# A decode block of attention and MLP on one core: two small side loads behind the fifth K unit, and a bias in one transfer

## Chip, core and metric

One core of a Trainium2 chip runs the program alone. The metric is the device time of one execution in microseconds (us), the median over several runs. Beside these times there is one profiled execution, with a record of every instruction and of every DMA packet. A core has TensorE (PE in the profile), VectorE (DVE), ScalarE (ACT), GpSimd (POOL) and SyncE (SP), and sixteen DMA engines that move the data. A transfer is issued on a queue, here SP's or ACT's, and is cut into packets that the DMA engines carry.

## What is computed

Two tokens (batch 2, one position, width 576) pass through a layer norm; then attention over a window of a key/value cache and an MLP run on the same normalized input, and both are added to `x`:

```python
def _A_ref(x, k_cache, v_cache, wq, wo):
    ...
    W = min(4096, max(256, Sk // 4))          # 2048 of 8192 positions
    q = (x @ wq)...                           # 32 heads of 128
    k = jnp.repeat(k_cache[:, :, Sk - W:, :], rep, axis=1)   # 16 kv heads, rep = 2
    v = jnp.repeat(v_cache[:, :, Sk - W:, :], rep, axis=1)
    scores = jnp.einsum("bhqd,bhkd->bhqk", q, k) * (Dh ** -0.5)
    p = _softmax(scores, axis=-1)
    o = jnp.einsum("bhqk,bhkd->bhqd", p, v)
    return ... @ wo

def _B_ref(x, w1, b1, w2, b2):
    h = jnp.einsum("bsd,df->bsf", x, w1) + b1                # 576 -> 4608
    r = jnp.where(h > zero, h, zero)
    return jnp.einsum("bsf,fd->bsd", r * r, w2) + b2

return x + _A_ref(xn, ...) + _B_ref(xn, ...)
```

All inputs are bf16. Some 53.6 MB are read: the windows of the K and V caches (16.8 MB each), `wq`, `wo` (4.7 MB each), `w1` and `w2` (5.3 MB each).

## The kernel before

The cache is cut into eight units (`NU = 8`), one for four kv heads of one batch row; a unit of K or V is a tile of 128 partitions with 16,384 bytes in each, loaded by one DMA (`issue_kv`, L105). Six such tiles (`kvpool`, `bufs=6`) are used in turn by K and V units. `wq`, `w1` and `wo` share one buffer (`wbig`, `issue_flat`, L118), so that `w1` can only be loaded after the queries are made, and `wo` only after the first MLP product.

Everything large is issued on SP's queue, in the order of the program: k0, wq, k1, v0, k2, v1, k3, v2, k4, v3, k5, v4, k6, v5, w1, k7, v6, v7, wo, and `w2` in five parts (w2a L435, w2b L436, w2c in three pieces L438, `W2P`). An SP issue waits for what its buffer's last user has to finish (PE, for a K or V tile), and for a semaphore: the transfers of the program take eight completion semaphores in turn, and a transfer can be issued only when the transfer that had the same semaphore eight places earlier has landed. ACT's queue carries the small ones: `x` (L124), the first MLP bias `b1_sb` (L415, three transfers of three, three and two rows of 1,152 bytes), the second bias (L416, one row) and half of the output (L474; L472 writes the same place once beforehand).

`step(u)` handles one unit: PE transposes K in eight groups (`kT_ps`, L96), ACT and DVE copy them to SBUF (L269, L271), `scores` and `softmax` follow, and the product with V of the unit two places back (`pv`, L93) lies between. `mlp_h` multiplies by `w1` (`h_ps`) after step 6, then the program issues `wo` and `w2`, runs step 7 and the last two `pv`, and sums everything into `out_ps`: first `wo` (tile `ws`), then `w2a`, `w2b`, three matmuls into an unused tile (`spin_ps`), and `w2c`. ACT copies `out_ps` to `fin_sb` (L473) and two DMAs write the output.

`w2c_sb` (L209) is allocated at the start, in a pool of its own, 128 partitions of nine rows of 576 numbers; it stays empty until the three pieces of L438 are loaded, late in the program.

Of the kernel before, what the change touches and what calls it, by code (L numbers as in the profile page):

```python
# [16 lines left out]
def kernel(  # L17
# [14 lines left out]
    nc = tc.nc  # L32
    P = 128
    B, Sq, D = A_x.shape
# [57 lines left out]
    def matmul(*a, **k):  # L92
        tc.keep_in_program_order(nc.tensor.matmul(*a, **k))  # L93
# [8 lines left out]
    def issue_kv(tiles, cache, u, name):  # L102
        tq, b = divmod(u, B)
        tl = kvpool.tile([P, UE], BF16, tag="kv", name=f"{name}_{u}")
        nc.sync.dma_start(out=tl[:], in_=cache[b, tq * TH:(tq + 1) * TH, S0:Sk, :].rearrange(  # L105
            "h (c j) d -> c h (j d)", c=CP))
        tiles[u] = tl

    def load_k(u):
        issue_kv(k_tiles, A_k_cache, u, "k")  # L110
# [67 lines left out]
    for t0, half, k0, n, pc in ((0, 0, 0, NK, 0), (0, 1, 0, NK, 1), (1, 0, 1, NK - 1, 1), (1, 1, 0, NK - 1, 0)):  # L178
# [11 lines left out]
                          in_=own[:].unsqueeze(2).to_broadcast([P, NC, WC]))  # L190
# [11 lines left out]
                          in_=ident[0:2 * NG4, 0:2 * NG4].rearrange("p (x g) -> p x g", g=NG4).unsqueeze(3)  # L202
# [5 lines left out]

    w2c_sb = w2pool.tile([P, (FR - R9) * D], BF16, name="w2c")  # L209

    out_ps = psum.tile([RO, HD], F32, tag="out", name="out_ps")
    nc.vector.memset(out_ps[:], 0.0)

    def out_acc(lhsT, rhs, o, start=False, stop=False, acc=out_ps, base=0):
        for i in range(2):
            p = base + 32 * i
            matmul(acc[p:p + B, :], lhsT=lhsT, rhs=rhs[:, o * D + i * HD:o * D + (i + 1) * HD], start=start,
                   stop=stop, skip_group_check=True, tile_position=(0, p))
# [165 lines left out]
    def step(u):  # L384
        fin = None
        w = u - 2
        with_pv = w >= 0
        for g in range(NG):
            transposes(u, g)
            if with_pv and g == 1:  # L390
                pv(w, 0, 2)
            if with_pv and g == 2:
                pv(w, 1, 2)
                fin = pv_end(w)
            if g == TG + 1:
                scores(u, 0)
            if g == TG + 2 and fin:
                fin()
        scores(u, 1)
        softmax(u)  # L400
# [10 lines left out]
    softmax(0)  # L411
    load_v(2)
    b1_rows = B_b1.rearrange("(x n) -> x n", n=HW)
    for i0, i1 in ((0, 3), (3, 6), (6, 8)):
        nc.scalar.dma_start(out=b1_sb[i0:i1, :], in_=b1_rows[i0:i1, :])  # L415
    nc.scalar.dma_start(out=xb_sb[B:B + 1, :], in_=B_b2.rearrange("(o n) -> o n", o=1))  # L416
    step(1)
    load_k(4)
    out_acc(sel_b[:], xb_sb, 0, start=True)
    for u in range(2, NU - 1):  # L420
        step(u)
# [84 lines left out]
```

## Time and profile before

| | |
|---|---|
| time, median of 3 runs | 133.90 us (133.72 to 133.91) |
| the profiled execution's own time | 133.77 us |
| its span | 131.9 us |
| PE busy | 86.9 us (66%) |
| DVE busy | 63.0 us (48%) |
| ACT busy | 46.7 us (35%) |
| DMA | 53.74 MB, mean 407 GB/s over the span |
| chain that ended last | DMA 77%, PE 17% |

The span goes from the program's first to its last instruction; the time has some 1.9 us more around it. The profile's views are: the busy time of each engine; the chain of work that ended last, followed back from the last instruction; busy time in stretches, with the share of the sixteen DMA engines that was busy; the queues with their packets; the waits of each queue; and, in the trace itself, each DMA packet with its queue, start, duration and size, and the landings of each transfer, sixteen for a transfer that all engines share.

The DMA share of the span in 40 equal slices, in tenths:

```profile
DMA  3999989999999999999999999999999989899970
```

### The profile page before, as it was taken

To read this page: it belongs to the slowest core of one execution; us is meant where nothing else is said; L and a number is where in the kernel's file an instruction comes from. 1 tells how busy PE (TensorE), PEld (TensorE's weight loads), DVE (VectorE), ACT (ScalarE), POOL (GpSimd) and SP (SyncE) were. 2 spreads that over 40 slices of the span, in tenths; PEclk is the share of its full clock that TensorE was granted. 3 is DMA by queue.
4 is the path that set the end of the run, shared out by engine and by line. 5 is a ranking of instruction groups with operands and counts; after the bars stand their busy time and mean duration, and the time that the engine had idled before them with its cause. 6 is when DMAs were issued, how large, how long until landed. Compare 5 with 4: busy or idle time off the path is not lost.

```text
span 131.9 us, 2023 instructions
## 1 busy us (share of the span) xinstructions
PE 86.9 (66%) x818; PEld 50.9 (39%) x818; DVE 63.0 (48%) x176; ACT 46.7 (35%) x68; POOL 4.2 (3%) x14
## 2 busy tenths in 40 slices
PE   0079419599589597599687699203919972729672
PEld 0069302287345353445353354002518630215241
DVE  6764400344657677457677457620072677550000
ACT  5715500339576094255094346010014532000101
POOL 2000000010010100100100100100010001000000
PEclk9999955959999999779999869855595999555999
DMA  3999989999999999999999999999999989899970
GB/s 120 432 443 493 403 383 427 407 462 403 455 412 442 427 407 462 407 442 427 432 437 400 457 479 428 407 415 423 427 427 442 504 374 492 380 421 399 409 285 1
DMA packets 3498, 53.74 MB, mean 407 GB/s; under 512 B 401, under 2 KB 546, under 8 KB 802
## 3 DMA queue, kind: packets, MB, share of 16 engines
q1 hardware_dynamic: 3460, 53.61, 95.4%
q8 instruction: 6, 0.10, 0.3%
q10 hardware_dynamic: 30, 0.02, 0.0%
q14 instruction: 2, 0.02, 0.0%
HBM read 53.62 MB, written 0.00 MB: 407 GB/s over the span
## 4 chain that ended last, share of the span: by engine, by line
DMA 77%; PE 17%; SPq 1%; DVE 1%; ACT 1%; issue 1%; ACTq 0%; DVEq 0%
DMA w<-in_B_w_dram 24%; DMA w2c<-in_B_w_dram 24%; DMA k<-in_A_k_cache_dram 16%; DMA wq<-in_A_wq_dram 13%; PE kT_ps L96 7%; PE h_ps L93 3%; PE q_ps L93 3%; PE sc_ps L93 1%; PE o_ps L93 1%; PE out_ps L93 1%; DVE qrow L237 1%; SPq L105 0%; ACT qrow L237 0%; DVE qz L253 0%; SPq L435 0%
## 5 line engine op out<-in xcount | busy, mean ns | idle before, releaser
L96 PE MATMUL kT_ps<-ident_f,k 128*128 128x128 f32 x256 | 42.0, 315 | 5.5 <-DMA k<-in_A_k_cache_dram 4.4
L96 PEld LDWEIGHTS kT_ps<-ident_f,k 128*128 128x128 f32 x256 | 33.3, 162 | 19.1 <-issue 10.2
L269 ACT COPY kT<-kT_ps 128x1024 bf16<-128x1024 bf16 x32 | 31.9, 1012 | 19.6 <-PE kT_ps L96 19.4
L271 DVE COPY kT<-kT_ps 128x1024 bf16<-128x1024 bf16 x32 | 21.8, 681 | 7.1 <-PE kT_ps L96 6.7
L93 PE MATMUL sc_ps<-kT,qz 128*32 128x512 bf16 x128 | 9.7, 383 | 6.7 <-DVE kT L271 4.7
L301 ACT ACTIVATE p<-sc_ps,bias 128x512 bf16<-128x512 f32 x8 | 5.5, 687 | 21.3 <-DVE gown L297 15.0
L93 PE MATMUL o_ps<-v,pT 128*32 128x512 bf16 x128 | 11.9, 455 | 0.0
L93 PEld LDWEIGHTS <-xnT 128*4 128x4 bf16 x108 | 3.6, 121 | 15.8 <-issue 14.2
L93 PE MATMUL h_ps<-w,xnT 128*4 128x288 bf16 x72 | 4.3, 431 | 7.2 <-DMA w<-in_B_w_dram 7.2
L304 DVE STREAM_TRANSPOSE pT<-p 128x512 bf16<-128x512 bf16 x8 | 5.7, 710 | 6.2 <-ACT p L301 6.2
L332 DVE SCALAR_TENSOR_TENSOR o<-o_ps,in_s,o 128x128 f32<-128x128 f32 x24 | 8.2, 344 | 0.4
L290 DVE TENSOR_REDUCE m<-sc_ps 128x1 f32<-128x512 f32 x8 | 5.5, 691 | 4.7 <-PE sc_ps L93 4.7
L93 PE MATMUL q_ps<-wq,xnT 128*4 128x512 bf16 x36 | 4.0, 628 | 4.6 <-DMA wq<-in_A_wq_dram 4.6
L372 DVE TENSOR_TENSOR hrow<-t 100x1152 bf16<-100x1152 f32 x2 | 2.6, 1355 | 8.9 <-ACT t L370 8.9
L93 PE MATMUL op_ps<-o,of_h 128*32 128x129 f32 x16 | 3.7, 316 | 4.6 <-DVE o L332 4.6
L93 PEld LDWEIGHTS <-qz 128*32 128x32 bf16 x128 | 2.1, 94 | 10.4 <-DVE kT L271 7.2
L294 POOL PARTITION_ALL_REDUCE gmax<-m x8 | 2.9, 366 | 93.6 <-DVE m L292 93.6
L96 PE MATMUL pro_ps<-ident,xn_sb 2*128 2x2 bf16 x5 | 0.9, 181 | 6.8 <-DVE xn_sb L169 6.5
L330 DVE TENSOR_SCALAR o<-o_ps,in_s 128x128 f32<-128x128 f32 x8 | 2.7, 342 | 4.7 <-PE o_ps L93 4.7
L458 ACT COPY pre_sb<-pre_ps 34x288 f32<-34x288 f32 x1 | 0.4, 393 | 12.6 <-PE pre_ps L93 12.6
L93 PE MATMUL out_ps<-wo,ws 128*2 128x288 bf16 x32 | 4.0, 443 | 1.1 <-DVE ws L348 1.1
L237 DVE CAST qrow<-q_ps 100x512 bf16<-100x512 f32 x1 | 0.7, 692 | 8.0 <-PE q_ps L93 8.0
(76 smaller groups left out, 61.2 us busy)
## 6 DMA issues: line engine op xcount, KB each, us to landing
k<-in_A_k_cache_dram SPq DMA_DIRECT2D x8, 2048.0 KB, 21.6
v<-in_A_v_cache_dram SPq DMA_DIRECT2D x8, 2048.0 KB, 33.6
w<-in_B_w_dram SPq DMA_DIRECT2D x1, 5184.0 KB
wq<-in_A_wq_dram SPq DMA_DIRECT2D x1, 4608.0 KB, 17.7
wo<-in_A_wo_dram SPq DMA_DIRECT2D x1, 4608.0 KB
w2a<-in_B_w_dram SPq DMA_DIRECT2D x1, 2592.0 KB
w2b<-in_B_w_dram SPq DMA_DIRECT2D x1, 1296.0 KB, 29.5
w2c<-in_B_w_dram SPq DMA_DIRECT2D x1, 864.0 KB
```

Of the source, the lines that this page charges most:

```text
L93: tc.keep_in_program_order(nc.tensor.matmul(*a, **k))
L96: tc.keep_in_program_order(nc.tensor.transpose(*a, **k))
L237: cp(out=qrow[:, k * QW:(k + 1) * QW].rearrange("p (i a d) -> p i a d", a=2, d=Dh), in_=q_ps[0:RB, k * QW // 2:(k + 1) * QW // 2].rearrang ...
L269: nc.scalar.copy(out=kT, in_=kT_ps[:])
L271: nc.vector.tensor_copy(out=kT, in_=kT_ps[:])
L290: nc.vector.tensor_reduce(out=m1[:], in_=sc_ps[:], axis=AX.X, op=ALU.max)
L294: nc.gpsimd.partition_all_reduce(gmax[:], m2[:], channels=P, reduce_op=ReduceOp.max)
L301: nc.scalar.activation(out=p_sb[:], in_=sc_ps[:], func=ACT.Exp, bias=bias[:, 0:1], scale=scale, accum_out=o1[:, Dh:Dh + 1])
L304: nc.vector.transpose(out=pT[:].rearrange("p j r -> p (j r)"), in_=p_sb[:])
L330: nc.vector.tensor_scalar(scalar1=in_s[:, 0:1], scalar2=None, op0=ALU.mult, **kw)
L332: nc.vector.scalar_tensor_tensor(scalar=in_s[:, k:k + 1], in1=o1[:, 0:Dh], op0=ALU.mult, op1=ALU.add, **kw)
L372: nc.vector.tensor_tensor(out=h4[:, :, k * HB:(k + 1) * HB], in0=t4, in1=t4, op=ALU.mult)
```

## The change

Two things are edited. The first MLP bias comes in one transfer of eight rows instead of three transfers. And after `load_k(4)` two transfers more are issued on SP's queue, by a new function `side_load(k, a0, c0)`. It reads from `w2`, seen as rows of 4,608 bytes (`w_rows`), `k` groups of six rows starting at row `a0`, of each group the first four; and writes them to `4 * k` partitions of `w2c_sb`, 4,608 bytes in each, from column `c0` on. `side_load(5, 0, 0)` fills partitions 0 to 19, `side_load(2, 32, 4 * D)` partitions 0 to 7 beside it. What they write is not read: the three pieces of L438 load all of `w2c_sb` as before. So 28 rows of 4,608 bytes, 0.13 MB, are read more.

```diff
     w2c_sb = w2pool.tile([P, (FR - R9) * D], BF16, name="w2c")
+
+    w_rows = B_w2.rearrange("(a r) n -> a (r n)", r=4)
+
+    def side_load(k, a0, c0):
+        nc.sync.dma_start(out=w2c_sb[0:4 * k, c0:c0 + 4 * D],
+                          in_=w_rows[a0:a0 + 6 * k, :].rearrange("(g i) n -> g i n", g=k)[:, 0:4, :])
...
     b1_rows = B_b1.rearrange("(x n) -> x n", n=HW)
-    for i0, i1 in ((0, 3), (3, 6), (6, 8)):
+    for i0, i1 in ((0, 8),):
         nc.scalar.dma_start(out=b1_sb[i0:i1, :], in_=b1_rows[i0:i1, :])
     nc.scalar.dma_start(out=xb_sb[B:B + 1, :], in_=B_b2.rearrange("(o n) -> o n", o=1))
     step(1)
     load_k(4)
+    side_load(5, 0, 0)
+    side_load(2, 32, 4 * D)
     out_acc(sel_b[:], xb_sb, 0, start=True)
```

The instructions of PE, DVE and POOL stay what they are, in the same order. ACT has two DMA issues less, SP two more. Because the completion semaphores are handed out in turn, the transfers behind the bias take other semaphores than before.

## The prediction

> **What bounds the kernel now.** I read the chain of waits first, then busy time by stretches, then the DMA queues, then what the SP queue waits for, and last the single DMA packets of the trace.
>
> ```profile
> 59.38 31.73 DMA w<-in_B_w_dram
> ...
> 91.14 4.35 PE h_ps L93 x72
> ...
> 96.84 31.09 DMA w2c<-in_B_w_dram
> 127.93 0.04 issue
> 127.97 1.37 PE out_ps L93 x18
> ```
>
> The columns are start, length, what. The end follows the last transfers: w2c, then 1.37 us of matmuls. The one stretch of computing in the last 70 us, 4.35 us of `h_ps`, counts only if the DMA engines run dry under it. The stretches say whether they do (last two columns: share of the 16 DMA engines that is busy, and GB/s):
>
> ```profile
> 2.50:20.00 17.50, 8.01 (x49) 6.70 (x53) 8.09 (x30) 7.41 (x10) 0.00 (x0) 0.90 0.99 420
> 20.00:60.00 40.00, 32.46 (x278) 18.99 (x270) 21.53 (x55) 19.10 (x29) 1.46 (x4) 0.87 1.01 430
> 60.00:91.00 31.00, 19.56 (x165) 10.22 (x164) 17.37 (x45) 11.99 (x16) 1.10 (x3) 0.85 1.00 429
> 91.00:125.00 34.00, 23.40 (x297) 13.16 (x297) 14.49 (x37) 6.66 (x13) 0.70 (x2) 0.74 1.00 429
> 126.50:127.00 0.50, 0.50 (x12) 0.35 (x7) 0.00 (x0) 0.00 (x0) 0.00 (x0) 1.00 0.93 362
> 127.00:127.25 0.25, 0.25 (x6) 0.11 (x2) 0.00 (x0) 0.00 (x0) 0.00 (x0) 1.00 0.68 270
> 127.25:127.50 0.25, 0.25 (x3) 0.12 (x2) 0.00 (x0) 0.00 (x0) 0.00 (x0) 1.00 0.45 171
> 127.50:128.00 0.50, 0.35 (x4) 0.05 (x4) 0.00 (x0) 0.00 (x0) 0.00 (x0) 1.00 0.46 176
> 128.00:128.50 0.50, 0.50 (x10) 0.36 (x11) 0.00 (x0) 0.00 (x0) 0.00 (x0) 1.00 0.36 127
> 128.50:128.75 0.25, 0.25 (x9) 0.22 (x6) 0.00 (x0) 0.00 (x0) 0.00 (x0) 1.00 0.04 14
> ```
>
> The engines are full from 2.5 to 125 us, at 429 to 430 GB/s from 20 us on. They do not stop together: from 127.25 us seven of sixteen (0.45) still work, from 128 six (0.36). The trace's landings of the last w2c piece show it one by one: eight engines between 127.28 and 127.61 us, two at 128.09, six between 128.75 and 128.99. The kernel ends when the slowest engine does, so the question is which engines are late, and why.
>
> ```profile
> q1 hardware_dynamic: 3460, 53.61, 95.4%
> q8 instruction: 6, 0.10, 0.3%
> q10 hardware_dynamic: 30, 0.02, 0.0%
> q14 instruction: 2, 0.02, 0.0%
> ```
>
> Six instruction fetches of 16,384 bytes (q8) and two of 8,192 (q14): six engines very late, two half late. In the packet records a q8 fetch starts where one engine's q1 packet ends (at 29.68, 48.90, 68.34, 84.53, 106.48 and 123.18 us), takes 0.88 to 0.96 us, and the q1 packet beside it grows from 0.61 to 1.09; after each, one more of the sixteen landings is some 1.5 us late. The q14 fetches (35.48 and 69.68 us) cost some 0.8. No engine is hit twice.
>
> **Which engine is hit.** Between two hits every engine sends one 16,384-byte packet each 0.607 us, so the sixteen keep their phases: 0, 29, 32, 34, 48, 52, 61, 70, 77, 116, 163, 169, 202, 213, 282 and 373 ns behind the earliest. The small ACT-queue packets (q10, 1,152 bytes) name three of them: the two b1 transfers of three rows put one packet on three engines each (8.80, 8.89, 8.94 us), the transfer of two rows on two of these (14.35, 14.49), the one-row b2 on one (17.12). Followed to the phases, engine "first" (four packets) is the one at 77, "second" (three) at 163, "third" (two) at 61. The q8 fetches hit 282, 48, 34, 70, 116 and one of 202 and 213; the q14 fetches 0 and 163. So first and third have slack, and **the second is one of the two that land at 128.09**.
>
> **The change, part by part.** *One b1 transfer instead of three.* ACT issues two DMAs less (0.98 us for three, before); its next work, `rstd`, leads to `xnT`, which waits for wq until 19.14 us anyway, so nothing is gained at the end. On the engines eight rows go one each to eight engines instead of 3, 3 and 2. One such packet costs its engine 0.053 us (the next q1 packet starts 47 ns late, and the one after the completion write 6). First and second save two, 0.11 us, third saves one, five others gain one. If b1 landed later, nothing is near: its matmul runs at 83.5 us.
>
> *The SP queue.* The semaphores of the transfers go round in order, eight in all, so two transfers less shift what each SP issue waits for.
>
> ```profile
> SPq L105 <- PE kT_ps L96: 29.9, 6, 9.3
> ...
> SPq L105 <- DMA k<-in_A_k_cache_dram: 12.1, 2, 7.1
> SPq L105 <- DMA b_sb<-in_B_b_dram: 6.4, 3, 2.3
> ```
>
> The 6.4 us of waiting for b1 go: v0, k2, v1 and k3 are issued sooner. v2 then waits for wq (19.14 us) and goes some 2.8 us later than its 16.37. Neither matters: at 19 us k1, v0, k2, v1 and k3 stand in the queues, 5 x 2.1 MB, 24 us at 430 GB/s. k4 (issued 33.41) waits for `kT_ps` as now. The two side loads are issued behind it, some 0.55 us each, before v3, whose own wait ends at 38.31: 4.4 us of room for 1.1. Behind v3 stand the later loads, each with 10 us and more of queue ahead of it. w1 will wait for k4's landing (54.54 us, issue at 59.38), k7 and v6 for the side loads' landing (about 55, issues at 62.61 and 67.20): all past by then. wo, issued after `h_ps` at 95.51, has cover until the v units land, 104.0 to 105.6 us. Cost: nothing.
>
> *The side loads themselves.* 20 + 8 packets of 4,608 bytes, read besides the full w2c load, which stays. Price: 53.61 MB in 95.4% of 16 x 131.9 us are 26.6 GB/s an engine, 0.173 us a packet. The trace has no transfer from a source in five groups. Bounds: spread evenly, 28 x 0.173 / 16 = 0.30 us on every engine; all on one engine, 4.8 us. The nearest rows are the small q10 transfers, one engine for each row of the outermost count; by them the outer counts five and two give five engines four packets each and the first two four more. I take that: 1.38 us on first and second, 0.69 on third, fourth and fifth, each with about 0.01 for completion writes. The engines have no pause, so each delay lasts to the end.
>
> The Trainium skill ("DMA: Bandwidth & Descriptors", "Why a DMA increments its semaphore by 16 and not by 1") says that a queue-issued DMA uses the largest number of engines up to 16 that divides both sides' outermost counts, the lowest-numbered ones; that would be the same five and two, and no side load in this trace shows it yet. The same page ("Specifications") gives about 27 GiB/s an engine, 0.159 us a packet as an estimate; with it the second engine's load would be 1.27 us and the sum below +0.27. The trace's 26.6 GB/s is what I use.
>
> *The sum.* Third: 127.31 (its place among the early eight) + 0.70 - 0.05 = 127.96, still early. First: 127.33 (likewise) + 1.39 - 0.11 = 128.6, just short of 128.99. **Second: 128.09 + 1.39 - 0.11 = 129.37, 0.38 us after today's last landing.** Fourth and fifth: unknown; +0.75 with their b1 row. What follows the last landing (`out_ps`, the copy, the output DMA) shifts along, since the matmuls already wait for w2c at 127.93. By the profiled execution (133.77 us, span 131.9, 1.9 around it) that is 134.15; the median of the three runs, 133.90, lies 0.13 above it, so 134.28.
>
> **The rivals.**
> *A, the forecast:* second sets the end, 134.3 (134.1 to 134.4 with the 0.2 us that the three runs differ).
> *B:* fourth or fifth engine is one of the six that q8 hits: 128.75 to 128.99 + 0.75 = 129.5 to 129.74, so +0.51 to +0.75, 134.4 to 134.65. For: six of the thirteen unnamed engines are hit; picked at random, the two are both spared in 7/13 x 6/12 = 0.27. Against: first, second and third are all spared by q8, which a run of neighbours explains better, and of eight such runs within the thirteen only two touch fourth or fifth.
> *N:* nothing to see, 133.8 to 134.1: the fetches fall on other engines when another program is loaded, and the five have slack. For: one profile can't show that places are fixed. Against: it takes 1.6 us of slack on first and second. With bad luck the same cause gives +1.3 (135.2).
> *F, faster:* the early stage is what gains. 2.5 to 20 us runs at 420 GB/s against 430, 17.5 x 10/430 = 0.41 us. If b1's small transfers and SP's waits for them cause this, most of it returns, 133.5; it decides once the early landings come over 0.3 us sooner and all loaded engines have slack. Against: the long packets of that stage (up to 1.17 us for 16,384 bytes) lie at 2.2 to 6 us, b1's packets at 8.8 and later.
>
> **How the numbers follow.** A 0.40, B 0.30, N 0.16, F 0.14. This kernel's measurement tells about 0.2%, 0.27 us, from no change: below 133.63 or above 134.17. A is above it four times in five (0.32), B always (0.30), N rarely (0.03): slower 0.65. Same: 0.08 of A, 0.12 of N, 0.02 of F: 0.22. Faster: 0.13. The range 133.7 to 134.7 takes in A, B and N, and leaves out F's larger half and N's bad luck, which is also the end towards 135 that the worst placing of the packets would give.
>
> **What will show it.** Landings of the last w2c piece: two landings about 0.38 us or more behind the old group of six, or (B) up to 0.75; the DMA share of stretches after 128.5 us above 0.04. The side loads as q1 packets of 4,608 bytes near 53 us at some 0.173 us each, and no idle DMA engine between 2.5 and 125 us. SP without waits for `b_sb`. I am wrong if the last landing stays at 129.0 us, if the q8 fetches name other engines, or if the whole bank lands earlier.

## The result, and the profile after

The changed kernel takes 134.05 us (median of 20 runs, 133.99 to 134.44), the kernel before 133.84 us on the same chips (20 runs, 133.64 to 133.98). The ratio is 1.0018 with a 95% interval of 1.0011 to 1.0025: about 0.2 us slower, clear of noise and small. The profiled execution took 134.00 us with a span of 132.1 us, against 133.77 and 131.9 before.

First the DMA queues of the changed kernel (packets, MB, share of 16 engines' span):

```profile
q1 hardware_dynamic: 3495, 53.74, 95.3%
q8 instruction: 6, 0.10, 0.3%
q10 hardware_dynamic: 30, 0.02, 0.0%
q14 instruction: 2, 0.02, 0.0%
```

q1 has 35 packets more, 28 of data and seven completion writes (packets of 4 bytes, one from each engine that has a share of a transfer): five for the first side load and two for the second. The fetches (q8, q14) are as many as before.

Then what SP does around the side loads (timeline of SP, start and length), and one line of its waits:

```profile
34.57 0.54 SPq L105 DMA_DIRECT2D k<-in_A_k_cache_dram  x1
35.15 1.70 SPq L214 DMA_DIRECT2D w2c<-in_B_w_dram  x2
39.47 0.58 SPq L105 DMA_DIRECT2D v<-in_A_v_cache_dram  x1
```

```profile
SPq L105 <- DMA b_sb<-in_B_b_dram: 1.8, 1, 1.8
```

The two issues take 1.70 us and lie in the pause before v3. Of the 6.4 us that SP waited for the bias 1.8 are left, and the time did not fall.

Last the end, by stretches (the last two columns are the share of the DMA engines that is busy, and GB/s), and the chain of waits:

```profile
127.00:127.25 0.25, 0.25 (x9) 0.18 (x5) 0.00 (x0) 0.00 (x0) 0.00 (x0) 1.00 0.86 346
127.50:128.00 0.50, 0.50 (x3) 0.17 (x2) 0.00 (x0) 0.00 (x0) 0.00 (x0) 1.00 0.56 217
128.00:128.50 0.50, 0.46 (x7) 0.25 (x7) 0.00 (x0) 0.00 (x0) 0.00 (x0) 1.00 0.54 199
128.50:128.75 0.25, 0.25 (x8) 0.18 (x6) 0.00 (x0) 0.00 (x0) 0.00 (x0) 1.00 0.26 92
128.75:129.00 0.25, 0.25 (x8) 0.19 (x5) 0.00 (x0) 0.00 (x0) 0.00 (x0) 1.00 0.05 16
```

```profile
96.86 29.32 DMA w2b<-in_B_w_dram
126.18 0.04 issue
126.22 1.27 PE out_ps L93 x18
127.49 0.64 PE spin_ps L93 x3
128.13 0.04 issue
128.18 1.37 PE out_ps L93 x18
129.54 0.02 issue
129.57 0.39 ACT fin_sb L481
```

From 128.0 to 128.5 us nearly nine engines (0.54 x 16) still work where six did (0.36), and from 128.5 to 128.75 us four (0.26) where fewer than one did (0.04). The matmuls of `w2c` end 0.20 us later (129.54 against 129.34). The sixteen landings of the last w2c piece, read from the trace, say it engine by engine (us):

```
before   127.28 .29 .30 .31 .33 .44 .47 .61 | 128.09 .09 | 128.75 .77 .80 .89 .98 .99
changed  127.32 .38 .62 .65 .71 .94 .98     | 128.69 .75 .76 .81 .96 129.05 .10 .15 .20
```

Eight early engines became seven, the pair at 128.09 is gone, and the late group has nine. The last landing went from 128.99 to 129.20, the last output landing from 131.06 to 131.28, the span from 131.89 to 132.11. So the whole difference is there before the output is written.

The landings carry no engine's name, but the packets show which engine is last. ACT's early write to the output (L480, two rows, queue q10) puts one packet on each of two engines, behind what these have queued. In the changed kernel the last data packet of q1 starts at 128.844 us, its completion write at 128.891, and 6 ns behind it, on the same engine, the second packet of that write (128.897); the next engine's completion write starts 0.13 us earlier, at 128.758. The early write's two landings come 0.16 to 0.18 us behind the last w2c landings of the two engines: before 127.49 and 128.27, for engines that end at 127.33 and 128.09; changed 128.87 and 129.37, for 128.69 and 129.20. So the last engine is one of these two. They are the two with eight side-load packets: with four packets more on each of those (below, "More on the pair") the two last landings are 129.38 and 129.84, and this write lands at 129.56 and 130.01. In this one execution other engines end close by, up to 129.15 where the latest was 128.99 before; that they don't set the loss is shown by the runs with parts of the change, not by this trace alone.

### The profile page after: what moved, and what is told of

Read it like the earlier page. It is cut to its first block, busy times and chain, and to the rows that moved or that the text cites. A ratio compares the mean times of both kernels' runs of the same rounds, so it can differ in the third digit from the quotient of the medians.

```text
span 132.1 us, 2023 instructions
## 1 busy us (share of the span) xinstructions
PE 87.7 (66%) x818; PEld 50.3 (38%) x818; DVE 62.8 (48%) x176; ACT 46.5 (35%) x68; POOL 4.2 (3%) x14
## 4 chain that ended last, share of the span: by engine, by line
DMA 76%; PE 17%; SPq 1%; ACT 1%; DVE 1%; issue 1%; ACTq 0%; DVEq 0%
DMA w<-in_B_w_dram 25%; DMA w2b<-in_B_w_dram 22%; DMA k<-in_A_k_cache_dram 15%; DMA wq<-in_A_wq_dram 13%; PE kT_ps L96 5%; PE h_ps L93 3%; PE q_ps L93 3%; PE sc_ps L93 2%; PE out_ps L93 2%; PE qT_ps L96 1%; SPq L105 1%; PE o_ps L93 1%; ACT kT L275 1%; DVE qrow L243 1%; PE spin_ps L93 0%
## 5 line engine op out<-in xcount | busy, mean ns | idle before, releaser
L96 PE MATMUL kT_ps<-ident_f,k 128*128 128x128 f32 x256 | 41.2, 311 | 5.3 <-DMA k<-in_A_k_cache_dram 2.7
L96 PEld LDWEIGHTS kT_ps<-ident_f,k 128*128 128x128 f32 x256 | 32.6, 159 | 19.3 <-issue 8.9
L93 PE MATMUL sc_ps<-kT,qz 128*32 128x512 bf16 x128 | 10.5, 414 | 6.5 <-DVE kT L277 4.7
```

The costliest lines, as they stand in the source:

```text
L96: tc.keep_in_program_order(nc.tensor.transpose(*a, **k))
```

## The experiments

Each run is compared with the kernel before on the same chip. "Last landing" is that of the last w2c piece in the profiled execution; "tail" is its span less the last landing of the output.

### The parts alone

The bias alone:

```diff
-    for i0, i1 in ((0, 3), (3, 6), (6, 8)):
+    for i0, i1 in ((0, 8),):
```

> The bias in one transfer, no side loads. Theory A (the end is set by the slowest DMA engine; first and second engine have slack before): the late six keep their place, change against before 0.0 us (within 0.1); SP no longer waits for the bias three times. Rival F (the bias transfers and SP's waits for them cost the early stage): 0.2 to 0.4 us faster than before. Rival G (the 0.13 MB read more cost bandwidth that all engines share, 129,024 bytes at 430 GB/s = 0.30 us, wherever they lie): 0.0, no side load here.

Measured: 134.01 us against 133.86, ratio 1.0011 (1.0002 to 1.0020). Last landing 129.08 (before 128.99), tail 0.96 us (before 0.82). F falls: merging the bias transfers brings no gain. The expected 0.0 was missed too, by 0.15 us, and most of it lies where no theory looked, in the tail. The second engine ends at 127.97 us here (read from ACT's early write, as above), where the prediction's sum without side loads has 128.09 - 0.11 = 127.98.

The side loads alone (the bias again in three):

```diff
-    for i0, i1 in ((0, 8),):
+    for i0, i1 in ((0, 3), (3, 6), (6, 8)):
```

> Both side loads, the bias in three transfers as before. Theory A: the second engine carries two bias packets more than in the changed kernel, 0.11 us, so 0.32 us over before. Rival F: the gain of the bias is missing, 0.4 to 0.6 us over before. Rival G: 0.30 us over before, no packet's place matters.

Measured: 134.41 against 133.86, 1.0045 (1.0032 to 1.0057). One landing stands alone at 129.44, 0.53 us behind the next (128.91); the tail is 1.00 us. The time, 0.55 us over before, misses A's 0.32 and by itself fits F, which the first run excludes. That one engine ends the kernel is as A says (it is the second again, by ACT's early write, which lands last at 129.62); its place is 0.13 us later than A's 129.31, and the tail adds 0.17.

The five groups alone:

```diff
     side_load(5, 0, 0)
-    side_load(2, 32, 4 * D)
```

> The side load of five groups alone (20 packets, four on each of five engines), bias in one transfer. Theory A: the second engine goes to about 128.09 + 0.70 - 0.11 = 128.7 us, the one of fourth and fifth that a small fetch hits to about 128.8, both before the late six (128.75 to 128.99): change against before 0.0 us (within 0.1). Rival G: 20 of 28 packets, 0.21 us slower than before.

Measured: 133.91 against 133.86, 1.0008 (0.9999 to 1.0017). Last landing 128.97, tail 0.90. Twenty packets more, and the last landing has not moved: these bytes alone cost nothing that shows, so G falls.

### More on the pair

```diff
     side_load(5, 0, 0)
     side_load(2, 32, 4 * D)
+    nc.sync.dma_start(out=w2c_sb[32:40, 0:4 * D],
+                      in_=w_rows[64:76, :].rearrange("(g i) n -> g i n", g=2)[:, 0:4, :])
```

> Both side loads and one more transfer of two groups (eight packets, four more on first and second engine, 36 in all). Theory A: every packet on the second engine now lies on the path, 4 x 0.174 = 0.70 us more than the changed kernel, 0.9 us over before. Rival G: 36 packets of 4,608 bytes at 430 GB/s, 0.39 us over before.

Measured: 134.89 against 133.86, 1.0079 (1.0065 to 1.0093): 1.03 us, A's 0.9 and not G's 0.39. The end of this run by stretches:

```profile
128.50:128.75 0.25, 0.18 (x1) 0.00 (x0) 0.00 (x0) 0.00 (x0) 0.00 (x0) 1.00 0.21 74
128.75:129.00 0.25, 0.18 (x4) 0.14 (x5) 0.00 (x0) 0.00 (x0) 0.00 (x0) 1.00 0.13 51
129.00:129.25 0.25, 0.25 (x8) 0.18 (x6) 0.00 (x0) 0.00 (x0) 0.00 (x0) 1.00 0.08 25
129.25:129.50 0.25, 0.25 (x8) 0.18 (x5) 0.00 (x0) 0.00 (x0) 0.00 (x0) 1.00 0.08 28
```

A share of 0.13 is two engines, 0.08 is one with a little of another: the pair that carries twelve packets each works on alone. Its landings are 129.38 and 129.84, the other fourteen end by 129.03. The last landing moved 0.64 us against the changed kernel for four packets of 0.174 us, 0.70: nearly one for one. The tail adds 0.11.

### The pair taken apart

The second engine's extra packets left out, the first keeps its four:

```diff
     side_load(5, 0, 0)
-    side_load(2, 32, 4 * D)
+    for i in range(4):
+        nc.sync.dma_start(out=w2c_sb[i:i + 1, 4 * D:8 * D], in_=w_rows[32 + i:33 + i, :])
```

> As the changed kernel, but the second side load's four packets on the second engine are left out: its four packets on the first engine come in four transfers of one row each. Theory A: the second engine ends at about 128.7 us, the first at 128.6, both before the late six: 0.0 to 0.1 us over before, so the changed kernel's loss is gone although 24 of its 28 packets stay. Rival G: 24 of 28 packets, 0.26 us over before.

Measured: 134.08 against 133.87, 1.0017 (1.0009 to 1.0026). By the time alone this is a miss for A and close to G. The profile says otherwise: the last landing is 128.99 and the last output landing 131.08, both as before (128.99, 131.06), yet the span is 132.15. All of it comes after the output has landed, in SP's wait at the program's end, here in the kernel before and in this run:

```profile
SPq L501 <- DMA out_dram<-fin_sb: 0.6, 1, 0.6
```

```profile
SPq L510 <- DMA out_dram<-fin_sb: 1.0, 1, 1.0
```

At the end SP waits for the completion semaphores one after another, some 0.06 us for each. The output's transfers hold the last of the eight in the kernel before; with more or fewer transfers they hold others, and waits that were done before the output now stand behind it. The tails agree over all runs (shift in number of transfers, tail): -2, 0.96; -1, 0.89 to 0.90 (four runs); 0, 0.82 to 0.84 (four); +1, 0.94; +2, 1.00; +3, 1.07; +4, 1.08. The change itself has two bias transfers less and two side loads more: shift 0, tail 0.83.

So the same question again with a shift of 0, one row of 10,368 bytes for the four:

```diff
     side_load(5, 0, 0)
-    side_load(2, 32, 4 * D)
+    nc.sync.dma_start(out=w2c_sb[40:41, :], in_=w2_rows[0, 0:1, 0:9 * D])
```

> As the changed kernel, but the second side load is one row of 10,368 bytes, on the first engine alone, so that second loses its four extra packets and the number of transfers, and with it the semaphores of the output, stay as in before and in the changed kernel. Theory A with the end's waits (the 0.2 us of the run with the first engine alone came from SP's last semaphore waits, not from a DMA engine): last landing 128.99 us within 0.1, last output landing to end of span 0.83 us, time 0.0 us from before (within 0.1). Rival G (bytes): 102,528 bytes at 430 GB/s, 0.24 us over before.

Measured: 133.86 against 133.84, 1.0002 (0.9993 to 1.0011), tail 0.83. The loss is gone with the second engine's four packets. The profiled execution of this kernel, 133.96 us, was the slowest of its eleven, with a last landing of 129.15. The two engines at issue are not the cause of that: ACT's early write lands at 128.57 and 128.67, so they end at about 128.4 and 128.5. For the time the medians decide.

### Where else

Eight groups, so that sixth to eighth engine get four packets too:

```diff
-    side_load(5, 0, 0)
-    side_load(2, 32, 4 * D)
+    side_load(8, 0, 0)
```

> One side load in eight groups in place of the two (32 packets, four on each of eight engines), bias in one transfer. Theory A: if one of sixth to eighth engine is among the six that the large fetches hit, it goes 0.70 us behind today's last (128.99), 0.7 to 0.8 us over before; if none is, no change (within 0.15 us). Rival G (cost by bytes alone): 32 packets, 0.34 us over before.

Measured: 134.41 against 133.87, 1.0044 (1.0032 to 1.0056). Two landings, 129.45 and 129.57, stand behind the rest (129.10): that fits two of sixth to eighth being engines that the large fetches hit, as the expectation's first branch has it. The size was 0.54 us, not 0.7 to 0.8, with 0.07 of it tail. It would fit that these two are not the latest of the six; that was not followed.

The side loads issued behind the seventh K unit:

```diff
     load_k(4)
-    side_load(5, 0, 0)
-    side_load(2, 32, 4 * D)
...
             load_k(u + 3)
+        if u == 3:
+            side_load(5, 0, 0)
+            side_load(2, 32, 4 * D)
```

> The changed kernel with its two side loads issued behind the seventh K unit instead of the fifth, the number of transfers as before. Theory A (what counts is the sum on the second engine, not the place in the queue): as the changed kernel, 0.2 us over before (0.1 to 0.35). Rival H (the loss comes from what the side loads hold up behind the fifth K unit): no loss, 0.0 us.

Measured: 134.00 against 133.84, 1.0014 (1.0005 to 1.0023): the changed kernel's loss within the intervals. (Its profiled execution, 134.22 us, was the slowest of its eleven; one landing, 129.42, stands 0.43 us behind the rest there, and by ACT's early write it is the second engine's.) H falls; the sum on an engine counts, not the place in the queue.

### The same packets on all sixteen

```diff
-    side_load(5, 0, 0)
-    side_load(2, 32, 4 * D)
+    nc.sync.dma_start(out=w2c_sb[0:32, 0:4 * D], in_=w_rows[0:32, :])
```

> The same 32 packets spread over all sixteen engines, two on each, bias in one transfer. Theory A and rival G alike: every engine, the late ones too, gets 0.35 us more, 0.35 us over before (0.35 to 0.5 with what the bias in one transfer showed). Beside the run with five groups (20 packets, no clear change) it shows what the same kind of packet costs where there is no slack.

Measured: 135.03 against 133.87, 1.0088 (1.0075 to 1.0101): 1.16 us, three times what either theory had. Every engine lands late, the earliest at 128.35 instead of 127.28. So 0.7 us had to be explained, and the next run is for it: as many bytes, laid over all 128 partitions.

```diff
-    side_load(5, 0, 0)
-    side_load(2, 32, 4 * D)
+    nc.sync.dma_start(out=w2c_sb[:, 0:D], in_=B_w2[0:P, :])
```

> One side load of the same 147 KB as the run over all sixteen engines, but to all 128 partitions with 1,152 bytes in each, as the other loads lie; bias in one transfer. Theory P (the run over sixteen engines lost 0.7 us more than its packets' time since sixteen engines wrote to the same 32 partitions): eight packets of 0.047 us on every engine, 0.39 us at the last landing, with the end's semaphore waits 0.4 to 0.55 us over before, and no long 16,384-byte packets behind it. Rival Q (a transfer more on all engines costs 1.1 us by itself): 1.0 to 1.2 us over before.

Measured: 134.28 against 133.84, 1.0032 (1.0021 to 1.0044), 0.44 us, as theory P has it (the last landing alone moved 0.26 us in the profiled execution, the fastest of its six, where 0.39 was expected). The stretch behind the side load in both runs, 32 partitions first, then 128:

```profile
52.50:54.50 2.00, 0.94 (x11) 0.20 (x9) 1.49 (x4) 0.44 (x1) 0.00 (x0) 1.00 1.04 327
54.50:56.00 1.50, 0.51 (x5) 0.54 (x6) 0.86 (x4) 0.00 (x0) 0.37 (x1) 1.00 0.96 362
```

```profile
52.50:54.50 2.00, 0.62 (x8) 0.12 (x8) 1.22 (x4) 0.00 (x0) 0.15 (x1) 1.00 1.10 457
54.50:56.00 1.50, 1.35 (x16) 0.98 (x16) 0.32 (x3) 0.96 (x3) 0.22 (x1) 1.00 1.10 470
```

The engines are busy in both, but at 327 and 362 GB/s in the first. Packets of 16,384 bytes behind the side load, which take 0.611 us elsewhere, take up to 1.19 us there; in the second run none takes more than 0.62. That the writes of sixteen engines to the same 32 partitions queue up fits this and was not separated from the other difference, the size of the rows.

### A try at a faster kernel

If late engines set the end, work should go from them to early ones:

```diff
+    r0, r1 = W2P[0]
+    for p0, p1 in ((112, 117), (117, 122), (122, 127), (127, 128)):
+        nc.sync.dma_start(out=w2c_sb[p0:p1, (r0 - R9) * D:(r1 - R9) * D], in_=w2_rows[1, p0:p1, r0 * D:r1 * D])
...
     for r0, r1 in W2P:
-        nc.sync.dma_start(out=w2c_sb[:, (r0 - R9) * D:(r1 - R9) * D], in_=w2_rows[1, :, r0 * D:r1 * D])
+        n = 112 if r0 == R9 else P
+        nc.sync.dma_start(out=w2c_sb[0:n, (r0 - R9) * D:(r1 - R9) * D], in_=w2_rows[1, 0:n, r0 * D:r1 * D])
```

> No side loads and the bias in three transfers as before; 16 of the 128 partitions of the first w2c piece (6,912 bytes in each) are carried by the first five engines, in three transfers of five rows and one of one row, right behind the fifth K unit; the piece itself has 112 partitions, seven packets an engine in place of eight. Theory A: the late six lose one packet of 0.262 us, 128.99 becomes 128.73; the second engine goes to 128.09 - 0.26 + 0.79 = 128.62 and stays before them: 0.26 us faster than before. Rival G (bytes alone, same bytes): no change.

Measured: 137.94 against 133.87, 1.0311 (1.0283 to 1.0339), 4.1 us slower: a clear miss.

```profile
123.00:125.00 2.00, 1.76 (x48) 1.00 (x40) 0.00 (x0) 0.00 (x0) 0.00 (x0) 0.72 1.00 414
125.00:127.00 2.00, 0.98 (x16) 0.18 (x6) 0.00 (x0) 0.39 (x1) 0.00 (x0) 1.00 1.02 237
127.00:129.00 2.00, 0.00 (x0) 0.00 (x0) 0.00 (x0) 0.00 (x0) 0.00 (x0) 1.00 1.02 224
```

With all engines busy the rate drops from 414 to 237 and 224 GB/s while the piece of 112 partitions is loaded: its packets of 6,912 bytes take 0.48 us on the mean and up to 0.81, against 0.262 in the kernel before. The packets of the five-row transfers, near 53 us, are slow too (0.26 to 0.57 us each). So the idea was not tested: the form that it took costs more than it could give. No version here beats the kernel before.

## Why the prediction was right, point by point

**The bound.** Right. The last landing of the slowest DMA engine sets the end: where it stayed (five groups alone, 128.97; first engine alone, 128.99) nothing but the tail moved the time, and where it moved (changed kernel, 0.21) the output followed by the same amount (0.22).

**Which engine.** Right. The second side load's four packets on the second engine are the loss: without them 1.0002 with the same number of transfers, with four more 1.0079. Less what the tail adds, the medians lie above before by 0.20 us (changed), 0.15 (issued later), 0.38 (side loads alone), 0.92 (four packets more), and by 0.01, -0.02, -0.03 and 0.01 in the four runs that leave these packets out (bias alone, five groups alone, first engine alone, one row). The first engine carries as much and has slack (time in hand before the last engine ends): it ends at 128.69. In the trace of the changed kernel the second small fetch (q14, 73.96 us) again meets one of the two engines that carry eight side-load packets: of the landings of one transfer after another, one moves from 1.34 us to 2.0 us behind the earliest across it.

**How the packets fall.** Right: five engines take four packets, two of them four more, 0.178 us long and 0.174 from start to start, against 0.173 predicted; the other estimate there, 0.159, is too short.

**The size.** 0.38 us were predicted for the last landing, 0.21 measured: right in kind, nearly twice too large. The term that was mis-sized is the second engine's place, 128.09, taken over from one execution with no spread. The eight packets cost what was summed (52.50 to 53.90 us, 1.40), and with the bias alone the engine ends where the sum has it (127.97 against 127.98), yet the changed kernel has it at 129.20 and not 129.37. Other runs give the spread. Measured end less the sum's is -0.05 us with the five groups alone (128.63), -0.07 with the eight groups (128.61), -0.04 with the side loads alone (129.44), +0.05 with the later issue (129.42) and -0.23 with four packets more (129.84). One part of that can be seen: the small fetch cost the engine 0.67 us in the trace of before and 0.55 in that of the changed kernel, where the packet that it meets was stretched to 0.85 us instead of 0.97. But it cost 0.55 in the run with the bias alone too, where the sum came out, so it isn't the whole account, and the rest stays open.

**The time.** 134.05 us lies just below the forecast's own 134.1 to 134.4 and inside rival N's 133.8 to 134.1, so the time alone would have spoken for N; the landings and the runs above decide for A. Part of it is the base: the kernel before measures 133.84 us here, not the 133.90 that the sum starts from. It also stays below the 134.17 that the prediction took as the least that can be told from no change; only the twenty runs of each kernel put 0.2 us clear of noise.

**The signs.** The side loads came as said, and after 128.5 us the DMA share lies above 0.04. "Two landings 0.38 us or more behind the old six" did not come, and did not follow from the sum either, which has only the second engine behind 128.99. The wait for `b_sb` shrank to 1.8 us and did not vanish.

**Rival B** (fourth or fifth engine hit by a large fetch) falls by the ends: it needs a landing at 129.5 us or later, 0.5 us over before, and the last is 129.20 in the changed kernel and 128.97 with the five groups alone, where these two engines carry the same. One of the five does lag: of the landings of the first side load four are at 53.49 to 53.55 us and one at 54.46, 0.9 behind, the size of a small fetch, which fits the other engine of the pair at 128.09; that one had room for its 0.75.

**Rival N** (places of the fetches change) falls for the second engine, which is the last one in the changed kernel, and finds no support otherwise: each kernel's trace has six large and two small fetches, and the runs that load the first five engines in different ways all fit the same places, the second with a small fetch and none of the five with a large one. The places of the other engines were not followed from run to run.

**Rival F** (the start gains) falls with the bias alone, 1.0011 (1.0002 to 1.0020) and not below 1.

**What cost nothing** cost nothing: SP's earlier issues, and the side-load issues before v3, which took 1.70 us and not 1.1. One detail of this step was wrong without effect: v2 was to wait for wq and go at 19.14 us, but the bias has the semaphore that v2 takes (landed at 10.75), v2 then waited for `kT_ps`, and went at 14.90. One thing was not seen: the end's semaphore waits. They cancel in the change (two transfers out, two in), and cost 0.07 to 0.25 us in the parts by themselves.

## What to carry to other kernels

When the DMA engines never pause, the end is set by one engine, not by the mean: read how many still work in the last microseconds and ask which of them a transfer with few rows is laid on. Here a load on engines with slack cost nothing, and four packets of 0.174 us on the wrong one cost 0.2 us, what was left of them beyond its slack. An engine's end worked out from one execution was off by up to 0.2 us, as much as this whole change. Where parts of a change are tried alone, watch that the number of transfers does not move the output to other semaphores, which looks like a cost of the part.

## What the runs showed of the hardware that was not expected

- An instruction fetch costs its DMA engine far more than its bytes (read before the change, and again in the traces of all runs): some 1.4 to 1.5 us for 16,384 bytes and 0.55 to 0.84 for 8,192, where a data packet of 16,384 takes 0.61. Each of the eight hit another engine in the trace of before, and the lag stays, with some 0.1 us lost on the way, to the end.
- SP's waits at the program's end take some 0.06 us each and stand behind the output or before it depending on the number of transfers: tails of 0.82 to 1.08 us.
- How rows meet engines matters as much as their number: 112 partitions on sixteen engines ran at 224 to 237 GB/s where 128 ran at 397 to 413 (kernel before, 123 to 127 us), and 32 rows on sixteen engines held up all of them by some 0.7 us beyond their own time. Why was not separated in either case.
